# VectorE transposes keys and queries from the 13th chunk; the steps of the inverses read rows; ScalarE scales rows and keys; VectorE makes all low halves

## The chip, the cores and the metric

The kernel runs on one core of one Trainium2 chip. The metric is the device time of one launch in microseconds (us). The engines are called by their names in the profile: PE is TensorE's matmul, PEld its weight load, DVE is VectorE, ACT is ScalarE, POOL is GpSimd, and SP is SyncE, which issues almost all DMAs.

## What is computed

Three layers in fp32: a gated delta rule over 768 steps for 4 batches x 8 heads of width 48, then two dense layers of 384 -> 2048 -> 384 over 3072 tokens, one with mish, one with hardswish.

```
k_n = k / (norm(k) + 1e-06)
for t in range(768):
    y[t]  = q[t] @ state
    v_old = k_n[t] @ state
    state = state + beta[t] * outer(k_n[t], v[t] - v_old)
x = y as (3072, 384)
h = x @ w_in;   x = (h * tanh(softplus(h))) @ w_out
h = x @ w2_in;  out = (h * clip(h + 3, 0, 6) / 6) @ w2_out
```

## The kernel before

**The recurrence** is cut into 24 chunks (t = 0 to 23) of 32 steps; (batch, step) fills the 128 partitions. For a chunk PE transposes keys and queries (`T_pe`, 4 transposes of 128x128 each, into PSUM; `T_ew` on ACT copies them into `kqt`), multiplies keys by keys and keys by queries (`G_pe`, into `gps`), and needs the inverse of the unit lower triangular matrix I + tril(beta K K^T), one 32x32 matrix for each batch and head. Then `rec()` runs, for each chunk in order: K (`ksps`, keys times state), r = v - K on DVE (L942), U (`ups`, inverse times r), its copy on ACT (L986), queries times state and MU (`yps`), S (`dsps`, the state's update) and eight additions into `sbd` on DVE (L890). The products of chunk t + 3 (G) go to PE with K of chunk t, the transposes of chunk t + 4 with U of chunk t.

The inverses of chunks 0 to 7 are made before by two blocks of substitutions (`whole`, `quads`). From chunk 8 on two chunks form a group g (4 to 11): `G_ew` on DVE multiplies the products by a lower mask times -beta (`mb`, made by `beta_mask` on POOL) into `an`; DMAs turn `an` through DRAM (`ad`) so that each partition holds a matrix (`ash`, [128, 32, 32]; its two halves of partitions solve for different columns); `substs` on DVE runs 31 steps, each a product (L785) into `tmp` and an addition (L792) into `tp`; DMAs turn `tp` back through DRAM (`td`) into `pt`, and `scale` on POOL (L813) multiplies `pt` by beta. `ash` and `tp` are single buffers. The upper product (keys by queries) is copied by ACT (`M_post`, L483) and masked by POOL (L622) into `mt`; for chunks 4 to 7 DVE does it from PSUM (`G_ew2`, L478).

**The dense layers** hold each fp32 operand as two halves in fp32r, a high one made by ACT and a low one by DVE (value minus high half), and run three matmuls for each product (`hps` L1205, `o` L1226, `p` L1364). Phase 1 (mish) makes six passes over blocks of 512 tokens, 16 units each; a pass needs four chunks of the recurrence. So phase 1 runs beside chunks 4 to 23. In its first pass the weights are also fetched and split: 28 pieces, for each ACT L1139, DVE L1141, L1144, L1147, L1150, ACT L1167, DVE L1170. The low half of a unit's activations (`glo`, L1245) is made by POOL in the first 16 units and by DVE in the other 80. Phase 2 (hardswish) follows, with no recurrence beside it.

**The order of work** is fixed when the program is built: `Flow` simulates the engines with estimated costs, and each part is a generator that yields either an event it needs or (engine, us). `pen` and `margin` are given by hand; `pen` is added to the part's start when the next instruction is picked. "DVE." marks work that the planner lets run beside POOL; plain "DVE" work it holds back while a POOL instruction runs. Every engine, and SP's queue of DMAs, runs its instructions in that order. PSUM banks are handed out by `room`.

## Time and profile before

| what | before |
|---|---|
| time, median of 3 runs | 1038.77 us (1038.46 to 1041.55) |
| the profiled execution's own time | 1040.45 us |
| its span in the trace | 1038.7 us |
| mean granted TensorE clock | 0.995 |
| PE busy | 1009.0 us (97%) |
| PEld busy | 842.5 us (81%) |
| DVE busy | 655.6 us (63%) |
| ACT busy | 452.0 us (44%) |
| POOL busy | 119.9 us (12%) |

The profiled execution is 1.75 us longer than its span and 1.68 us above the median. Busy time of PE holds overlaps: a matmul of 512 columns is shown as about 0.39 us long, while the next one starts 0.23 us after it, so PE shows as busy whenever its queue is not empty. The other engines' busy time is closer to occupation. The shares are means over a start of 88.5 us, phase 1 beside the recurrence, and phase 2.

### The profile page before, as it was taken

The page shows a single profiled execution, that of the slowest core. Times are in us where ns is not written, and L with a number is a line of the kernel's source. Part 1 is how long each engine was busy: PE and PEld are TensorE (multiplying, and loading weights), DVE is VectorE, ACT ScalarE, POOL GpSimd, SP SyncE. Part 2 cuts the span into 40 slices and gives each one's busy share as a digit, 9 for nine tenths or more (in the row PEclk, how much of TensorE's full clock was granted, in tenths as well). Part 3 has the DMA queues.
Part 4 walks back from the last instruction along what each step waited for, and adds up shares of the span by engine and source line. Part 5 has one row for each costly group of instructions (what it writes and reads, how often), then busy time and mean ns, then how long its engine had stood idle before and what let it go on. Part 6 is the DMA issues. An engine that isn't in the chain of part 4 may idle for free.

```text
span 1038.7 us, 29553 instructions
## 1 busy us (share of the span) xinstructions
PE 1009.0 (97%) x12708; PEld 842.5 (81%) x12730; DVE 655.6 (63%) x1569; ACT 452.0 (44%) x916; POOL 119.9 (12%) x156
## 2 busy tenths in 40 slices
PE   8888999999999999999999999999999999999997
PEld 5466777787777878878778888998999989999997
DVE  7988999976869598596628888333343333433432
ACT  4454666534454354444236665333343333433432
POOL 3242333303121221210000000000000000000000
PEclk9999999999999999999999999999999999999999
DMA  4644553234242434414113643002020020100101
GB/s 87 158 97 103 152 129 99 78 57 77 42 95 41 76 54 87 74 20 89 22 44 121 203 137 107 1 1 62 1 61 1 1 61 1 37 25 1 31 1 32
DMA packets 149124, 66.58 MB, mean 64 GB/s; under 512 B 133088, under 2 KB 136160, under 8 KB 148992
## 3 DMA queue, kind: packets, MB, share of 16 engines
q1 hardware_dynamic: 147664, 64.19, 25.8%
q8 instruction: 100, 1.64, 0.7%
q10 hardware_dynamic: 1328, 0.49, 0.2%
q14 instruction: 32, 0.26, 0.1%
HBM read 51.02 MB, written 13.63 MB: 62 GB/s over the span
## 4 chain that ended last, share of the span: by engine, by line
PE 72%; DVE 16%; issue 2%; ACT 2%; DMA 1%; POOL 0%; SPq 0%; DVEq 0%; ACTq 0%
PE hps L1205 32%; PE p L1364 19%; PE o L1226 12%; DVE tmp L785 3%; DVE sbd L890 3%; DVE tp L792 3%; DVE cv L1147 1%; DVE cv L1150 1%; PE tps L434 1%; PE ksps L827 1%; PE ups L837 1%; PE yps L847 1%; PE dsps L879 1%; PE yps L827 1%; DVE glo L1245 1%
## 5 line engine op out<-in xcount | busy, mean ns | idle before, releaser
L1205 PE MATMUL hps<-xh,wih 128*128 128x512 f32 x576 | 229.5, 398 | 4.7 <-DVE an L472 1.8
L1205 PE MATMUL hps<-xl,wih 128*128 128x512 f32 x576 | 227.5, 395 | 2.3 <-DVE xl L1187 2.2
L1205 PE MATMUL hps<-xh,wil 128*128 128x512 f32 x576 | 227.3, 395 | 0.0
L1339 DVE SCALAR_TENSOR_TENSOR r<-r,hps 128x512 f32<-128x512 f32 x96 | 66.1, 688 | 181.6 <-ACT r L1337 181.4
L1337 ACT ACTIVATE r<-hps,half_c 128x512 f32<-128x512 f32 x96 | 66.1, 689 | 174.8 <-PE hps L1205 174.8
L1205 PEld LDWEIGHTS hps<-xh,wih 128*128 128x128 f32 x576 | 108.7, 189 | 27.5 <-DVE an L472 3.1
L1364 PE MATMUL p<-woh,glo 128*128 128x384 f32 x384 | 129.5, 337 | 0.0
L1364 PE MATMUL p<-woh,ghi 128*128 128x384 f32 x384 | 129.2, 337 | 0.0
L1364 PE MATMUL p<-wol,ghi 128*128 128x384 f32 x384 | 128.9, 336 | 0.0
L1205 PEld LDWEIGHTS hps<-xl,wih 128*128 128x128 f32 x576 | 108.7, 189 | 24.3 <-DVE xl L1187 5.0
L1205 PEld LDWEIGHTS hps<-xh,wil 128*128 128x128 f32 x576 | 108.6, 188 | 23.1
L1236 ACT ACTIVATE g<-hps 128x512 f32<-128x512 f32 x96 | 57.3, 597 | 132.0 <-PE hps L1205 130.2
L1226 PE MATMUL o<-ghi,wol 128*128 128x512 f32 x288 | 114.2, 396 | 0.1
L1226 PE MATMUL o<-ghi,woh 128*128 128x512 f32 x288 | 113.6, 394 | 0.0
L1345 DVE TENSOR_TENSOR glo<-r,ghi 128x512 fp32r<-128x512 f32 x96 | 66.5, 693 | 60.8 <-ACT ghi L1211 60.2
L1245 DVE TENSOR_TENSOR glo<-g,ghi 128x512 fp32r<-128x512 f32 x80 | 56.3, 704 | 75.4 <-ACT ghi L1211 75.0
L1211 ACT ACTIVATE ghi<-r 128x512 fp32r<-128x512 f32 x96 | 60.6, 632 | 70.4 <-DVE r L1339 70.4
L785 DVE TENSOR_TENSOR tmp<-tp,ash 128x126 f32<-128x126 f32 (+22 forms) x248 | 84.8, 342 | 8.8 <-DMA ash<-ad 2.5
L1226 PE MATMUL o<-glo,woh 128*128 128x512 f32 x288 | 84.3, 394 | 0.0
L1364 PEld LDWEIGHTS p<-woh,ghi 128*128 128x128 f32 x384 | 72.2, 188 | 4.0
L1364 PEld LDWEIGHTS p<-wol,ghi 128*128 128x128 f32 x384 | 72.1, 188 | 3.9
L792 DVE TENSOR_TENSOR tp<-tp,tmp 128x126 f32<-128x126 f32 (+22 forms) x248 | 69.3, 279 | 6.5
(148 smaller groups left out, 1384.0 us busy)
## 6 DMA issues: line engine op xcount, KB each, us to landing
raw<-in_moe_w_in_dram SPq DMA_DIRECT2D x24, 512.0 KB, 3.6
raw<-in_moe_w_out_dram SPq DMA_DIRECT2D x32, 384.0 KB, 3.2
vt<-in_v_dram SPq DMA_DIRECT2D x96, 48.0 KB, 2.4
x2d<-x2out SPq DMA_DIRECT2D x6, 768.0 KB, 3.8
x2in<-x2d SPq DMA_DIRECT2D x6, 768.0 KB, 5.5
kpad<-in_k_dram SPq DMA_DIRECT2D x92, 48.0 KB, 2.3
qpad<-in_q_dram SPq DMA_DIRECT2D x88, 48.0 KB, 2.5
ash<-ad SPq DMA_DIRECT2D x16, 256.0 KB, 4.0
```

The costliest lines, as they stand in the source:

```text
L785: nc.vector.tensor_tensor(out=tv, in0=x[:, 0:m, j:j + 1].to_broadcast([128, m, n]), in1=a[:, j + 1:C, j:j + 1].rearrange("p i o -> p o i") ...
L792: nc.vector.tensor_tensor(out=x[:, 0:m, j + 1:C], in0=x[:, 0:m, j + 1:C], in1=tv, op=ALU.add)
L890: nc.vector.tensor_tensor(out=o, in0=o, in1=S_part(b, r), op=ALU.add)
L1205: nc.tensor.matmul(out=ps[0], lhsT=w[:, kk, c], rhs=xhl[n][xi][:, kk, :], start=(kk == 0 and x == 0), stop=(kk == KD - 1 and x == 2))
L1211: nc.scalar.activation(out=hi, in_=g, func=ACTF.Copy)
L1226: nc.tensor.matmul(out=acc[i][dc], lhsT=w[:, e, 128 * dc:128 * (dc + 1)], rhs=a, start=(f == 0 and x == 0), stop=(f == KF - 1 and x == 2))
L1236: nc.scalar.activation(out=g, in_=ps, func=ACTF.Mish)
L1245: (nc.gpsimd if u < KF else nc.vector).tensor_tensor(out=lo, in0=g, in1=hi.bitcast(F32), op=ALU.subtract)
L1337: nc.scalar.activation(out=r, in_=ps, func=ACTF.Relu, scale=1.0 / 6.0, bias=half_c)
L1339: nc.vector.scalar_tensor_tensor(out=r, in0=r, scalar=1.0, in1=ps, op0=ALU.min, op1=ALU.mult)
L1345: nc.vector.tensor_tensor(out=lo, in0=r, in1=hi.bitcast(F32), op=ALU.subtract)
L1364: nc.tensor.matmul(out=acc[n][s], lhsT=a[:, c], rhs=w[:, e, :], start=(f == 0 and x == 0), stop=(f == KF - 1 and x == 2))
```

## The change

From chunk 12 on (`TD`) PE no longer transposes. `loads_q` fetches keys and queries of a chunk a second time (keys are still fetched in the old layout for S), each with four DMAs, into the two buffers `qpad` so that every 32x32 block holds steps by components; `turns` on DVE transposes such blocks, one instruction of 512 elements in each partition for keys and one for queries, straight into `kqt`, whose layout becomes [batch, head pair, 2, 32]. The columns that pad 48 to 64 are set to zero once by two memsets on POOL.

The matrix to be inverted is now I + tril(K K^T) diag(beta). ACT copies the raw product into `an` and multiplies it by beta with one instruction for each head (8, in place); the steps in `substs` read row j of `ash` where they read column j, and subtract; nothing masks `an`. The inverse is not multiplied by beta any more (POOL's L813 goes). Beta enters the upper product instead (POOL's mask becomes upper mask times beta) and the keys that update the state (`scale_k`, 8 instructions of ACT for each chunk, in place, after the chunk's key norms and, below chunk 12, after its transposes; S waits for it). `rec` no longer waits for the mask of chunk t + 3.

The fetch of `ash` moves into a part of its own (`fetches`): once all weights of phase 1 are split, odd groups use another buffer, and `tp` moves to a pool with two buffers. For chunks 4 to 7 the upper product goes to ACT and POOL (`M_early`) instead of DVE. All 96 low halves of phase 1 are made by DVE. Several `pen`s and `margin`s of the planner are set anew, and some cost estimates.

```diff
+        def raw_kq(i):
+            return qpad[i].rearrange("p j r d -> p (j r d)").rearrange("p (n x) -> p n x", x=C)
+
         def loads_q():
-            for t in range(4, NS):
+            for t in range(4, TD):
                 yield f"Tq{t - NQP}"
                 yield LOAD
                 load_q(t)
+            for t in range(TD, NS):
+                yield f"S{t - 5}"
+                for i, src in ((0, k), (1, q)):
+                    yield f"Tq{TD - 2 + i}" if t == TD else f"kqt{t - 1}.{i}"
+                    x = raw_kq(i)
+                    if t == TD:
+                        yield "POOL", 0.5
+                        for r in range(2):
+                            nc.gpsimd.memset(x[64 * r + 32:64 * r + 64, :, 16:32], 0.0)
+                    yield LOAD
+                    for r in range(2):
+                        for d0, d1 in ((0, 32), (32, D)):
+                            nc.sync.dma_start(
+                                out=x[64 * r + d0:64 * r + d0 + C, :, 0:d1 - d0],
+                                in_=src[:, r::2, C * t:C * (t + 1), d0:d1].rearrange("b j s d -> s (b j) d"),
+                            )
+                    flow.ev[f"raw{t}.{i}"] = flow.landed(3.0)
+
+        def turns():
+
+            for t in range(TD, NS):
+                yield f"QS{t - NKQ}"
+                for i in range(2):
+                    yield f"raw{t}.{i}"
+                    yield "DVE.", 0.705
+                    if i == 0:
+                        kqt[t] = ap_.tile([128, B, NP, 2, C], F32, tag=f"kqt{t % NKQ}", name="kqt")
+                    nc.vector.transpose(out=kqt[t].rearrange("p b j i s -> p (b j) i s")[:, :, i, :], in_=raw_kq(i))
+                    flow.set(f"kqt{t}.{i}")
+                flow.set(f"kq{t}")
...
-        def beta_mask(t, tag="mb"):
-            m = ap_.tile([128, H, C], F32, tag=tag, name="mb")
+        def beta_mask(t, tri):
+            m = ap_.tile([128, H, C], F32, tag="mb", name="mb")
             nc.gpsimd.tensor_tensor(
                 out=m,
-                in0=maskl.rearrange("p (o c) -> p o c", o=1).to_broadcast([128, H, C]),
...
-                kqt[t] = ap_.tile([128, NP, B, 2, C], F32, tag=f"kqt{t % NKQ}", name="kqt")
+                kqt[t] = ap_.tile([128, B, NP, 2, C], F32, tag=f"kqt{t % NKQ}", name="kqt")
             nc.scalar.activation(
                 out=kqt[t][:, :, :, i, :],
-                in_=tps.pop((t, i)).rearrange("p j (b s) -> p j b s", b=B),
+                in_=tps.pop((t, i)).rearrange("p j (b s) -> p b j s", b=B),
                 func=ACTF.Copy,
...
-                for r in range(2):
-                    yield "DVE.", 0.28, 0
-                    G_ew2(t, r)
-                    release(("G", t, r))
-                flow.set(f"mt{t}")
+                yield from M_early(t)
...
-            flow.add(M_post(t), pen=-0.227)
+            flow.add(M_post(t), pen=-0.202)
+            g, tt = divmod(t, 2)
+            if tt == 0:
+                an[g] = ap_.tile([128, 2, H, C], F32, tag="an", name="an")
+            x = an[g][:, tt]
             for r in range(2):
-                yield "DVE.", 0.285
-                G_ew(t, r)
+                yield "ACT", 0.28
+                nc.scalar.activation(out=x[:, r::2, :], in_=gps[t, r][:, :, 0:C], func=ACTF.Copy)
                 flow.set(f"an{t}.{r}")
-            if t % 2:
+            yield f"n{t}"
+            for h in range(H):
+                yield "ACT", 0.23, 0
+                nc.scalar.activation(out=x[:, h, :], in_=x[:, h, :], func=ACTF.Copy, scale=bnat[:, t, h:h + 1])
+            if tt:
                 yield "SP", 0.45
-                g = t // 2
                 an[g], x = drp.tile([2 * H, B * C, C], F32, tag="ad", name="ad", bufs=2), an[g]
                 nc.sync.dma_start(out=an[g].rearrange("p s j -> s p j"), in_=x.rearrange("s t h j -> s (t h) j"))
...
                 release(("G", t, r))
+            yield f"mb{t}"
             yield "POOL", 0.74
-            nc.gpsimd.tensor_tensor(out=m, in0=m, in1=masku.rearrange("p (o c) -> p o c", o=1).to_broadcast([128, H, C]),
-                                    op=ALU.mult)
+            nc.gpsimd.tensor_tensor(out=m, in0=m, in1=mbs[t], op=ALU.mult)
             flow.set(f"mt{t}")
+
+        def scale_k():
+
+            for t in range(8, NS):
+                if t < TD:
+                    yield f"Tq{t}"
+                yield f"n{t}"
+                for h in range(H):
+                    yield "ACT", 0.28, 0
+                    x = kdata(t)[:, h, :]
+                    nc.scalar.activation(out=x, in_=x, func=ACTF.Copy, scale=bnat[:, t, h:h + 1])
+                flow.set(f"ks{t}")
         def T_post(t, i):
             yield "ACT", 0.6
             T_ew(t, i)
...
-        def substs():
+        ash = {}
+
+        def fetches():
             for g in range(4, NGR):
                 yield f"ad{g}"
-                yield lock("ash")
+                own = "lo1.27" in flow.ev
+                tag = "r1" if own and g % 2 else "ash"
+                yield lock(tag)
                 yield "SP", 0.9
                 d = an[g].rearrange("p (b s) j -> (p b) (s j)", b=B)
-                a = ap_.tile([128, C, C], F32, tag="ash", name="ash")
-                x = ap_.tile([128, C // 2, C], F32, tag="tp", name="tp")
+                if tag == "r1":
+                    a = cvp.tile([128, 512, 2], F32, tag="r1", name="ash").rearrange("p n t -> p (n t)")
+                    a = a.rearrange("p (s j) -> p s j", j=C)
+                else:
+                    a = ap_.tile([128, C, C], F32, tag="ash", name="ash")
                 for hf in range(2):
                     nc.sync.dma_start(out=a[64 * hf:64 * hf + 64].rearrange("p s j -> p (s j)"), in_=d)
-                at = [flow.landed(2.5)]
+                at = flow.landed(2.5)
+                if own:
+                    x = x2p.tile([128, 512], F32, tag="x2", name="tp").rearrange("p (c i) -> p c i", i=C)
+                else:
+                    x = ap_.tile([128, C // 2, C], F32, tag="tp", name="tp")
                 yield "POOL", 0.75
                 nc.gpsimd.memset(x, 0.0)
                 xf = x.rearrange("p c i -> p (c i)")
                 for hf in range(2):
                     nc.gpsimd.memset(xf[64 * hf:64 * hf + 64, hf::34], 1.0)
-                yield lambda: at[0]
+                ash[g] = a, x, tag
+                flow.ev[f"ash{g}"] = max(at, flow.cur)
+
+        def substs():
+
+            for g in range(4, NGR):
+                yield f"ash{g}"
+                a, x, tag = ash.pop(g)
                 for j in range(C - 1):
                     n, m = C - 1 - j, j // 2 + 1
-                    yield "DVE", 0.165 + 0.00175 * n * m
+                    us = 0.165 + 0.00106 * n * m
+                    yield "DVE", us
                     t = ap_.tile([128, 256], F32, tag="tmp", name="tmp")
                     tv = t[:, 0:m * n].rearrange("p (m n) -> p m n", n=n)
                     nc.vector.tensor_tensor(
-                        out=tv,
-                        in0=x[:, 0:m, j:j + 1].to_broadcast([128, m, n]),
-                        in1=a[:, j + 1:C, j:j + 1].rearrange("p i o -> p o i").to_broadcast([128, m, n]),
-                        op=ALU.mult,
-                    )
-                    yield "DVE", 0.165 + 0.00098 * n * m
-                    nc.vector.tensor_tensor(out=x[:, 0:m, j + 1:C], in0=x[:, 0:m, j + 1:C], in1=tv, op=ALU.add)
-                give("ash")
+                        out=tv, in0=x[:, 0:m, j:j + 1].to_broadcast([128, m, n]),
+                        in1=a[:, j:j + 1, j + 1:C].to_broadcast([128, m, n]), op=ALU.mult)
+                    yield "DVE", us
+                    nc.vector.tensor_tensor(out=x[:, 0:m, j + 1:C], in0=x[:, 0:m, j + 1:C], in1=tv, op=ALU.subtract)
+                give(tag)
                 yield "SP", 0.9
                 d = drp.tile([2 * H, B * C, C], F32, tag="td", name="td", bufs=2)
                 for hf in range(2):
@@ -809,12 +867,6 @@
             yield flow.landed(1.5) - flow.cur
             pt[g] = x
             for t in range(2):
-                yield "POOL", 0.62
-                nc.gpsimd.tensor_tensor(
-                    out=x[:, t], in0=x[:, t],
-                    in1=bnat[:, 2 * g + t, :].rearrange("p (h o) -> p h o", o=1).to_broadcast([128, H, C]),
-                    op=ALU.mult,
-                )
                 flow.set(f"pt{2 * g + t}")
...
-                tk = t + 4 if 4 <= t < NS - 4 else None
+                tk = t + 4 if 4 <= t < TD - 4 else None
...
-                        yield f"mb{tg}"
...
+                if 8 <= t and not last:
+                    yield f"ks{t}"
...
-            yield ("POOL", 1.29) if u < KF else ("DVE", 0.69)
-            (nc.gpsimd if u < KF else nc.vector).tensor_tensor(out=lo, in0=g, in1=hi.bitcast(F32), op=ALU.subtract)
+            yield "DVE", 0.69
+            nc.vector.tensor_tensor(out=lo, in0=g, in1=hi.bitcast(F32), op=ALU.subtract)
...
-            due = flow.ev["moe1"] + 24.438 * (idx // 7) - 2.164 * max(1, end - idx + 1)
-            return 0.025 if due - flow.free["DVE"] < 2.89 else 0.128
+            due = flow.ev["moe1"] + 23.341 * (idx // 7) - 2.164 * max(1, end - idx + 1)
+            return -0.044 if due - flow.free["DVE"] < 2.886 else 0.055
...
-        flow.add(rec(), margin=busy(0.0, 1.05))
+        flow.add(whole(), pen=-0.324)
+        flow.add(rec(), margin=busy(0.0, 0.916))
...
+        flow.add(turns(), pen=0.078)
...
-        flow.add(quads(1), pen=busy(0.305, -0.161), margin=busy(0.0, 1.077))
+        flow.add(scale_k(), pen=busy(0.54, 0.003))
+        flow.add(quads(1), pen=busy(0.251, 0.007), margin=busy(0.0, 1.077))
+        flow.add(fetches(), pen=-0.111)
         flow.add(substs(), pen=0.008)
...
         for _ in range(2):
             flow.add(w1.lane(), pen=w1_pen)
```

## Rows read from the trace of the kernel before

**Rows 1.** The page's head: busy time of the engines.

```profile
PE 1009.0 (97%) x12708; PEld 842.5 (81%) x12730; DVE 655.6 (63%) x1569; ACT 452.0 (44%) x916; POOL 119.9 (12%) x156
```

**Rows 2.** Windows, phase 1's first four passes: us; PE, PEld, DVE, ACT, POOL busy.

```profile
88.50:195.00 106.50, 102.22 (x2105) 80.95 (x2105) 99.27 (x233) 62.19 (x144) 37.63 (x34) 0.98 0.47 123
195.00:290.00 95.00, 92.39 (x1604) 73.66 (x1603) 72.13 (x220) 42.60 (x101) 16.69 (x22) 0.98 0.29 59
290.00:385.00 95.00, 93.18 (x1610) 74.50 (x1609) 70.12 (x222) 41.49 (x101) 18.62 (x23) 1.00 0.36 68
385.00:477.00 92.00, 91.29 (x1610) 74.12 (x1609) 68.49 (x213) 43.40 (x108) 16.33 (x25) 1.00 0.37 70
```

**Rows 3.** Chain of waits by line: stretch 89 to 195, 290 to 385, 385 to 477.

```profile
by line: DVE cv L1147 12.3%; DVE cv L1150 10.7%; issue 10.5%; DVE sbd L890 10.3%; DVE cv L1141 6.3%; DVE wol L1170 6.0%; DVE tmp L785 5.9%; DVE tp L792 5.2%; DVE wil L1170 4.2%; PE hps L1205 3.6%; DVE cv L1144 3.3%; DMA raw<-in_moe_w_in_dra
by line: DVE tmp L785 14.4%; DVE tp L792 12.3%; DVE sbd L890 11.5%; PE hps L1205 11.1%; PE o L1226 9.8%; issue 5.9%; DMA ash<-ad 4.9%; DVE glo L1245 4.6%; POOL nn L414 4.5%; SPq L797 2.1%; ACT vt L342 2.0%; PE ksps L827 1.8%; PE gps L454 1.
by line: PE hps L1205 36.5%; PE o L1226 33.7%; PE tps L434 4.5%; PE dsps L879 3.8%; PE ksps L827 3.7%; PE ups L837 3.5%; PE yps L847 3.5%; PE gps L454 3.4%; PE yps L827 3.0%; PE xps L1041 2.1%; issue 0.7%; DVE tmp L785 0.7%; DVE r L942 0.6%
```

**Rows 4.** Timeline of PE around the transposes of one chunk, near 398 us.

```profile
398.52 0.66 PE L434 MATMUL tps<-ident,kpad 128*128 128x128 f32 x4
399.01 0.60 PE L434 MATMUL tps<-ident,qpad 128*128 128x128 f32 x4
399.37 0.48 PE L1226 MATMUL o<-ghi,wol 128*128 128x512 f32 x1
```

**Rows 5.** Groups by line: busy us, mean ns of one, idle before.

```profile
L785 DVE TENSOR_TENSOR tmp<-tp,ash 128x126 f32<-128x126 f32 (+22 forms) x248 | 84.8, 342 | 8.8 <-DMA ash<-ad 2.5
L792 DVE TENSOR_TENSOR tp<-tp,tmp 128x126 f32<-128x126 f32 (+22 forms) x248 | 69.3, 279 | 6.5
L472 DVE TENSOR_TENSOR an<-gps,mb 128x128 f32<-128x128 f32 x32 | 8.7, 283 | 2.5 <-ACT mt L483 2.5
L440 ACT ACTIVATE kqt<-tps 128x512 f32<-128x512 f32 x48 | 27.1, 595 | 17.8 <-PE tps L434 17.2
L342 ACT ACTIVATE vt<-vt,nn 128x48 f32<-128x48 f32 x144 | 36.2, 322 | 0.6 <-DMA vt<-in_v_dram 0.5
L483 ACT ACTIVATE mt<-gps 128x128 f32<-128x128 f32 x40 | 9.1, 272 | 34.8 <-PE gps L454 34.8
L1245 POOL TENSOR_TENSOR glo<-g,ghi 128x512 fp32r<-128x512 f32 x16 | 23.4, 1462 | 47.3 <-ACT ghi L1211 36.4 <-issue 10.9
L1245 DVE TENSOR_TENSOR glo<-g,ghi 128x512 fp32r<-128x512 f32 x80 | 56.3, 704 | 75.4 <-ACT ghi L1211 75.0
L641 DVE STREAM_TRANSPOSE late<-late 128x1024 f32<-128x1024 f32 x1 | 1.2, 1246 | 0.0
L718 DVE STREAM_TRANSPOSE late<-late 128x1024 f32<-128x1024 f32 x1 | 1.9, 1929 | 0.0
```

**Rows 6.** Timeline of POOL and DVE near 94 to 98 us.

```profile
94.61 1.29 POOL L1245 TENSOR_TENSOR glo<-g,ghi 128x512 fp32r<-128x512 f32 x1 [6.07 <-ACT ghi L1211]
94.79 1.53 DVE L1150 SCALAR_TENSOR_TENSOR cv<-raw,cv 128x384 uint32<-128x384 uint32 x1
98.07 0.55 DVE L1150 SCALAR_TENSOR_TENSOR cv<-raw,cv 128x384 uint32<-128x384 uint32 x1
```

**Rows 7.** Timeline of ACT: seven instructions of the value scaling in a row.

```profile
333.03 1.68 ACT L342 ACTIVATE vt<-vt,nn 128x48 f32<-128x48 f32 x7
```

**Rows 8.** Chain of waits in order of time, from 301 to 309 us.

```profile
301.16 1.36 SPq L797
...
304.02 4.61 DMA ash<-ad
```

**Rows 9.** Timeline of SP: four DMAs of one chunk's queries.

```profile
225.41 1.80 SPq L268 DMA_DIRECT2D qpad<-in_q_dram  x4
```

**Rows 10.** Timeline of POOL and ACT: an inverse scaled, then the copy of U.

```profile
218.60 1.19 POOL L813 TENSOR_TENSOR pt<-pt,bnat 128x256 f32<-128x256 f32 x2 [3.25 <-DMA pt<-td]
223.63 0.49 ACT L986 ACTIVATE u<-ups 128x384 f32<-128x384 f32 x1 [2.98 <-PE ups L837]
```

More of the change, by code (lines that the diff above doesn't have):

```diff
@@ L21 @@
 NKQ = 4
+TD = 12
 RATE, TOKENS = 32.0, 110.0
@@ L553, in matrix @@
             yield "POOL", 0.62
-            beta_mask(t)
+            beta_mask(t, maskl)
             yield 0.05
@@ L827, in state_pe @@
                     nc.tensor.matmul(
-                        out=ps[C * b:C * (b + 1), j, :], lhsT=kqt[t][:, j, b, i, :], rhs=sbd[:, b, j, :],
+                        out=ps[C * b:C * (b + 1), j, :], lhsT=kqt[t][:, b, j, i, :], rhs=sbd[:, b, j, :],
                         start=(i == 0 or j == 0), stop=(i == 0), skip_group_check=True,
@@ L932, in rec @@
                         G_pe(tg)
-                        flow.add(G_post(tg), pen=0.029, back=0.4 if tx and x1 else 0.0)
+                        flow.add(G_post(tg), pen=0.046, back=0.4 if tx and x1 else 0.0)
                     if tx and x1:
@@ L1577, in tile_delta_rule__moe_mish__moe_hardswish @@
             flow.add(w1.lane(), pen=w1_pen)
-        flow.add(moe(), pen=0.292)
+        flow.add(moe(), pen=0.321)
         flow.add(phase2())
```

31 lines of the change are left out of this document (13 added, 18 removed).

## The prediction

> **What bounds the kernel now.** I read the head of the page first, then busy time by stretch, then the chain of waits, then PE's timeline. The head shows PE busy for 97% of the span and no other engine above 63% [rows 1]. A mean hides the stages, so the next view cuts phase 1 at the starts of its passes [rows 2]. In the first pass PE is idle for 106.50 - 102.22 = 4.3 us and DVE for 106.50 - 99.27 = 7.2 us: both are nearly full. In the second to fourth pass, 282 us, PE is idle for 282 - 276.86 = 5.1 us, DVE for 71 us, ACT for 154 us. The chain of waits says who sets the pace [rows 3]: in the first pass it runs over DVE's splitting of weights (L1147, L1150, L1141, L1170), in the third largely over DVE's inverse steps (L785, L792) and state additions (L890) with PE's dense matmuls between, in the fourth over PE almost alone, and 4.5% of that stretch are the transposes (L434) that the change removes. So from 195 us on PE is full, with the inverses close behind; before that DVE is.
>
> **PE's transposes.** They go for chunks 12 to 23, 12 blocks of 8. One block goes from 398.52 to the next matmul at 399.37, 0.85 us from start to start [rows 4]; its busy time would count overlaps. 12 x 0.85 = 10.2 us. All 12 blocks stand beside U of chunks 8 to 19, in the stretch where PE is full. The dense matmuls behind them move up, so I take the whole 10.2 us; the bounds are nothing (if another engine sets the pace) and 10.2.
>
> **What DVE gets in return.** Two transposes of 512 elements for each of 12 chunks. The trace has none of this shape; 1024 dense elements take 1.25 us, and 1.93 us where one side is strided [rows 5]. Half of the dense one is 0.62, the full strided one 1.93; I take 0.70, near the dense row, since blocks of 32 stay dense: 24 x 0.70 = 16.8 us, at most 46. Against it stand the two products of each chunk into `an` (L472, 0.283), 32 x 0.283 = 9.1 us, and the step's product, which by reading rows should cost what the addition costs: 248 x (342 - 279) ns = 15.6 us [rows 5]; the bounds are nothing and that. From 195 to 477 us this is about 24 x 0.70 - 24 x 0.283 - 13.7 = -3.7 us for DVE. It lies in DVE's 71 us of idle time; even at 1.93 each (+26 us) it would fit. Without that cover it would cost what it takes.
> The row on PE's side is 0.85 us for a chunk's transposes, on DVE's side about 1.4 us, and ACT's two copies of 0.595 us go too [rows 4, 5]. The Trainium skill ("VectorE: DVE Perf Modes", Rules for kernel authors) speaks against the change: for a full 128x128 transpose it says to use TensorE where PSUM will do as destination. By that rule the sum would lose, 16.8 us for 10.2; by the rows it gains, because PE is the full engine after 195 us and DVE is not.
>
> **The inverses.** Between two groups DVE had no step to run: after one group's result is written (1.36 us of SP) the next fetch of `ash` takes 4.61 us, both on the chain [rows 8]. With two buffers the fetch is early. The scaling of the result on POOL also goes, 1.19 us for two, and U comes some 5 us after it starts [rows 10]. So pauses and late inverses become rarer; what is late next is PE itself. I give half of PE's 5.1 us of idle time in these passes as regained, 2.5 us; bounds 0 and 5.1.
>
> **ACT.** Each chunk from 8 on gets 2 copies of 0.272 us (L483's shape), 8 scalings of 128x32 and 8 of 128x48. The latter shape takes 0.322 us alone, but seven in a row take 1.68 us, (1.68 - 0.322) / 6 = 0.226 us apart [rows 5, 7]. For 128x32 the bounds are 0.15 (by elements) and 0.322; I take 0.226. A chunk: 2 x 0.272 + 2 x (7 x 0.226 + 0.322) = 4.35 us. From 195 to 477 us 13 chunks add 56.6 us and 24 copies of 0.595 go (14.3): 42 on 127.5, so 170 of 282 us. It is hidden by ACT's idle time. New waits: S waits for the scaled keys, U's copy can queue behind a run of 1.9 us; PE has dense matmuls for such a time, so I cost it at nothing, and at 1.9 us for each chunk if it has none.
>
> **The first pass.** DVE gets 16 low halves of 0.704 us, 11.3 us; it loses the 8 products of chunks 4 to 7 and the 6 of chunks 8 to 10 (0.283 each, 4.0 us) [rows 5]. That is +7.3 us on 99.27, the whole stretch. But POOL's 16 low halves, 23.4 us, also slowed DVE: the same instruction (L1150) took 1.53 us beside one and 0.55 us later [rows 6]. The relief is between nothing and 16 x 0.98 = 15.7 us; I take half, 7.8, as not every POOL half met such work. Net -0.5 us of DVE: nothing. ACT there gets 8 x 0.272 + 3 x 4.35 = 15.2 us on 62.19. I count the first pass as unchanged; bounds: 4.3 us shorter (PE's idle time) to 22 us longer (below).
>
> **SP's queue and DMA.** For chunks 12 on eight DMAs replace the four of the queries. Four take 1.80 us of SP, 0.45 each [rows 9], so four more make +1.8 us for each chunk; at 1.36 each, as one of a write of `td` took [rows 8], +9.1. Behind them in SP's order stand the transfers of the inverses, keys and values. A chunk lasts some 24 us (95 / 4), so I cost it at nothing. POOL's masks change in kind only; two memsets come once.
>
> **Sum.** -10.2 - 2.5 + 0 = -12.7 us. The profiled execution took 1040.45 us in all, its span and 1.75 us around it; it would take 1027.75. That execution lies 1.68 us above the median, so for the median 1038.77 - 12.7 = 1026.1 us. Start, last passes and phase 2 are left as they are: PE alone fills phase 2.
>
> **Rivals.** *More is regained.* The inverses no longer hold anything up and the first pass loses its 4.3 us: -10.2 - 5.1 - 4.3 = -19.6, 1019.2 us. For it speaks the chain in the third pass and the first; against it that PE's idle time is spread over many small waits. Chance 0.15.
> *SP falls behind.* If the short rows of keys and queries make each DMA cost 1.36 us of SP, 12 chunks are each delayed by up to 9.1 us in their inverses; PE covers most of it with dense matmuls until the block of tokens runs out at a pass's end. At about 1.5 us in each of four passes it gives back 6 us and nothing is regained: 1038.77 - 10.2 + 6 = 1034.6. Against it: 0.45 is what such DMAs take. Chance 0.13.
> *TensorE is not the bound.* The chain of the third pass runs more over DVE than over PE [rows 3]; if the inverses' loop sets the pace, PE waits where it transposed, and only the regained 2.5 us are left: 1036.3 us, no change. Against it: PE's idle time is only 5.1 of 282 us, and in the fourth pass the chain is PE. The Trainium skill ("Perfetto Trace Analysis", Identifying the Most-Contended Engine) bears on this: matmul busy time overstates how full TensorE is, the share of weight loads tells better. PEld is busy for 222.3 of these 282 us, 79% [rows 2], and by that rule PE has a fifth to spare and the rival holds; no row here shows such spare time as waits. Chance 0.09.
> *The first pass gets longer.* The place is ACT and DVE between 88.5 and 195 us, where the chain is DVE's splitting of weights with ACT at both its ends. If there is no relief from POOL, DVE needs 106.6 us and keeps its 7.2 us of waits: +7.3; if the 15.2 us of small ACT instructions also stand ahead of the splitting, the pass grows by up to 22 us: 1038.77 - 10.2 + 22 = 1050.6. It decides once the pass grows by more than 10.2 + 3.1. For it: both engines' work grows where they are the chain; against it: ACT has 44 us of idle time there, and the POOL row. Chance 0.08.
>
> **How the numbers follow.** The forecast as summed, 1021 to 1031.5 us, has 0.55; the rivals 0.15, 0.13, 0.09 and 0.08. A measurement here can tell 0.3%, 3.1 us. Faster: 0.55 + 0.15 + 0.13 = 0.83; same 0.09; slower 0.08. The range for 8 in 10 takes in the first two rivals: 1018 to 1036.
>
> **What would show it.** PE's L434 should lose 96 instructions and the time from the start of the second pass to that of the fifth should shrink by 10 us or more; L785's mean should equal L792's; DVE transposes should take about 0.70 us; in the first pass L1150 should have no instruction near 1.5 us beside a low half. Wrong would be: the chain of the second to fourth pass moving to ACT's scalings or SP's issues, PE waiting for `kqt`, or a first pass well over 106 us.

## The result, and the profile after

The changed kernel takes 1026.4 us (median of 4 runs, 1024.99 to 1028.12), the kernel before in the same comparison 1040.16 us; the ratio is 0.9863, 95% interval 0.9828 to 0.9899. In a second comparison it was 0.9882 (0.9854 to 0.9910). That is 12.3 to 14.2 us (the two intervals together reach from 9.4 to 17.9), and 1026.1 us was forecast. The forecast's sum held; the experiments below show that its terms did not all hold. A trace shows a single execution, which can lie some us off its kernel's median (in two of the experiments below, 1042.0 against 1037.34 us in e5 and 1045.9 against 1043.81 in e4), so lengths of passes read from one trace are good to some us only.

The head of the page of the changed kernel, which answers to [rows 1]:

```profile
span 1023.5 us, 29655 instructions
PE 996.6 (97%) x12620; PEld 831.4 (81%) x12620; DVE 640.6 (63%) x1569; ACT 496.4 (49%) x1188; POOL 88.3 (9%) x132
```

The shares hardly move; only ACT gains (452.0 to 496.4 us) and POOL loses (119.9 to 88.3). Where the time went is seen by passes. A pass is here taken from ACT's first high half of its block of tokens to that of the next, the first pass from the first dense matmul. Busy time of the changed kernel's first five passes (us; PE, PEld, DVE, ACT, POOL; then the granted clock, DMA share and GB/s), which answers to [rows 2]:

```profile
83.70:189.90 106.20, 100.75 (x2204) 79.23 (x2201) 100.11 (x252) 80.12 (x238) 21.52 (x27) 0.98 0.48 126
189.90:281.10 91.20, 89.17 (x1579) 71.20 (x1578) 67.13 (x213) 51.20 (x158) 15.15 (x21) 1.00 0.42 75
281.10:370.20 89.10, 88.71 (x1581) 71.22 (x1580) 69.23 (x224) 54.03 (x174) 14.03 (x19) 1.00 0.47 82
370.20:461.40 91.20, 89.49 (x1582) 72.14 (x1581) 65.39 (x203) 50.24 (x156) 11.55 (x16) 1.00 0.42 74
461.40:544.80 83.40, 83.40 (x1229) 67.39 (x1229) 51.84 (x138) 34.04 (x61) 0.00 (x0) 1.00 0.20 62
```

Cut in the same way, the kernel before starts its first dense matmul at 89.0 us and its passes take 103.2, 97.2, 94.7, 92.8 and 83.9 us:

```profile
89.00:192.20 103.20, 99.09 (x2078) 78.74 (x2075) 96.63 (x224) 60.31 (x140) 36.79 (x32) 0.98 0.48 125
192.20:289.40 97.20, 94.50 (x1612) 74.95 (x1611) 74.17 (x225) 43.88 (x105) 17.31 (x22) 0.98 0.29 57
289.40:384.10 94.70, 92.88 (x1609) 74.27 (x1608) 69.92 (x221) 41.19 (x101) 17.89 (x24) 1.00 0.35 67
384.10:476.90 92.80, 92.09 (x1613) 74.80 (x1612) 69.29 (x216) 44.20 (x108) 17.23 (x25) 1.00 0.37 70
476.90:560.80 83.90, 83.63 (x1230) 67.26 (x1229) 52.04 (x132) 32.71 (x59) 3.28 (x4) 1.00 0.18 52
```

So the start is 5.3 us earlier, the first pass 3.0 us longer, the second to fourth are 6.0, 5.6 and 1.6 us shorter (13.2 together, where 10.2 + 2.5 were forecast), the fifth 0.5; the rest differs by 0.8 us the other way.

About 1.7 us of the second pass's 6.0 are TensorE's clock. In the kernel before PE is busy for only 1.31 and 1.19 of 2 us in the stretches from 194 and 196 us, and in the next two, from 198 to 202 us, the granted clock is 0.52 and 0.62, near the lower of its two levels (1.00 is 2.4 GHz, 0.50 is 1.2 GHz); 2 x 0.48 + 2 x 0.38 = 1.7 us is an estimate of what that costs. In the changed kernel the granted clock is 1.00 in every such stretch from 100 to 490 us. So here a wait of TensorE at a pass's end was followed by a loss of about its own size.

The chain of waits by line in the first pass (84 to 190 us) and the third (281 to 370 us) of the changed kernel, which answers to [rows 3] (the view ends its lines where they end here):

```profile
by line: PE hps L1258 19.1%; PE o L1279 15.4%; PE qps L776 6.2%; DVE sbd L942 5.2%; issue 4.7%; DVE cv L1203 4.1%; DVE cv L1200 3.7%; POOL nn L448 3.7%; ACT an L638 3.2%; ACT kqt L474 2.4%; PE gps L488 2.3%; DVE wil L1223 2.2%; ACT wih L122
by line: PE hps L1258 35.8%; PE o L1279 33.2%; PE ksps L879 3.6%; PE gps L488 3.5%; DVE sbd L942 3.1%; PE dsps L931 2.9%; PE yps L899 2.7%; PE ups L889 2.7%; DVE tp L850 2.2%; PE yps L879 2.2%; PE xps L1094 2.2%; DVE tmp L846 1.7%; issue 1.
```

The third pass was DVE's (inverse steps 14.4% and 12.3%) and is now PE's: the steps have 1.7% and 2.2%. In the first pass DVE's splitting of weights (L1200 and L1203, before L1147 and L1150) falls from 23% to 8%, PE's dense matmuls (L1258, before L1205) rise from 3.6% to 19.1%, and ACT's scalings (L638) appear.

Groups by line (busy us, mean ns of one, idle before), which answer to [rows 5]: PE's transposes before, then the changed kernel:

```profile
L434 PE MATMUL tps<-ident,kpad 128*128 128x128 f32 x100 | 16.6, 290 | 0.0
L434 PE MATMUL tps<-ident,qpad 128*128 128x128 f32 x88 | 13.5, 275 | 0.7 <-DVE r L942 0.7
```

```profile
L468 PE MATMUL tps<-ident,kpad 128*128 128x128 f32 x52 | 9.9, 318 | 0.2
L468 PE MATMUL tps<-ident,qpad 128*128 128x128 f32 x40 | 6.1, 276 | 0.0
L354 DVE STREAM_TRANSPOSE kqt<-qpad 128x512 f32<-128x512 f32 x24 | 17.0, 707 | 0.1
L846 DVE TENSOR_TENSOR tmp<-tp,ash 128x126 f32<-128x126 f32 (+22 forms) x248 | 65.6, 264 | 12.5 <-POOL tp L831 4.3 <-DMA ash<-ad 2.1
L850 DVE TENSOR_TENSOR tp<-tp,tmp 128x126 f32<-128x126 f32 (+22 forms) x248 | 65.7, 265 | 7.1
L666 ACT ACTIVATE kpad<-kpad,bnat 128x48 f32<-128x48 f32 x128 | 32.1, 324 | 17.0 <-DVE bnat L416 17.0
L1298 DVE TENSOR_TENSOR glo<-g,ghi 128x512 fp32r<-128x512 f32 x96 | 66.6, 694 | 66.2 <-ACT ghi L1264 65.5
```

The prices were right: a transpose on DVE takes 0.707 us (0.70 forecast), the step's product costs as much as its partner (264 and 265 ns), a scaling of the keys 0.324 us. PE's transposes fall from 100 to 52 for keys and from 88 to 40 for queries, 96 in all. The longest instruction of the weights' splitting (L1203, before L1150) falls from 1.67 to 1.31 us, where none near 1.5 us was expected.

ACT's timeline (six scalings of 128x32, then eight of 128x48) and SP's (the new loads of one chunk) in the second pass:

```profile
227.23 1.37 ACT L638 ACTIVATE an<-an,bnat 128x32 f32<-128x32 f32 x6
232.08 1.92 ACT L666 ACTIVATE kpad<-kpad,bnat 128x48 f32<-128x48 f32 x8 [3.11 <-DVE bnat L416]
```

```profile
237.20 2.93 SPq L339 DMA_DIRECT2D qpad<-in_k_dram  x4
240.23 2.66 SPq L339 DMA_DIRECT2D qpad<-in_q_dram  x4
```

A run of eight takes 1.92 us, as summed; the narrower ones come (1.37 - 0.325) / 5 = 0.21 us apart, 0.325 being the median of one alone. A DMA of the new kind takes SP 0.67 to 0.73 us in this chunk and 0.48 to 0.86 over all 12 chunks, between the 0.45 taken and the bound of 1.36. The chunk's transposes on DVE (L354) have 0.1 us of idle time before them in all, so the loads are early enough.

### The profile page after: what moved, and what is told of

Its sections match the earlier page's. It is cut to its first block, busy times and chain, and to the rows that moved or that the text cites. A ratio compares the mean times of both kernels' runs of the same rounds, so it can differ in the third digit from the quotient of the medians.

```text
span 1023.5 us, 29655 instructions
## 1 busy us (share of the span) xinstructions
PE 996.6 (97%) x12620; PEld 831.4 (81%) x12620; DVE 640.6 (63%) x1569; ACT 496.4 (49%) x1188; POOL 88.3 (9%) x132
## 4 chain that ended last, share of the span: by engine, by line
PE 85%; DVE 10%; ACT 3%; issue 2%; POOL 0%; DMA 0%; SPq 0%; DVEq 0%; ACTq 0%
PE hps L1258 37%; PE p L1417 20%; PE o L1279 17%; PE dsps L931 2%; PE ups L889 1%; PE ksps L879 1%; PE gps L488 1%; DVE sbd L942 1%; PE yps L899 1%; DVE tw L700 1%; PE yps L879 1%; DVE late L707 1%; PE xps L1094 1%; DVE tmp L846 1%; DVE cv L1200 1%
## 5 line engine op out<-in xcount | busy, mean ns | idle before, releaser
L1258 PE MATMUL hps<-xh,wih 128*128 128x512 f32 x576 | 229.5, 399 | 2.6 <-ACT mt L510 1.3
L1258 PE MATMUL hps<-xh,wil 128*128 128x512 f32 x576 | 226.7, 394 | 0.7 <-issue 0.7
L1258 PE MATMUL hps<-xl,wih 128*128 128x512 f32 x576 | 226.5, 393 | 0.0
L1258 PEld LDWEIGHTS hps<-xh,wih 128*128 128x128 f32 x576 | 108.4, 188 | 26.6 <-issue 2.7
L1258 PEld LDWEIGHTS hps<-xh,wil 128*128 128x128 f32 x576 | 108.3, 188 | 23.2
L1258 PEld LDWEIGHTS hps<-xl,wih 128*128 128x128 f32 x576 | 108.4, 188 | 19.2
L1298 DVE TENSOR_TENSOR glo<-g,ghi 128x512 fp32r<-128x512 f32 x96 | 66.6, 694 | 66.2 <-ACT ghi L1264 65.5
L1398 DVE TENSOR_TENSOR glo<-r,ghi 128x512 fp32r<-128x512 f32 x96 | 66.5, 693 | 60.8 <-ACT ghi L1264 60.3
L846 DVE TENSOR_TENSOR tmp<-tp,ash 128x126 f32<-128x126 f32 (+22 forms) x248 | 65.6, 264 | 12.5 <-POOL tp L831 4.3
L1417 PEld LDWEIGHTS p<-woh,glo 128*128 128x128 f32 x384 | 72.0, 188 | 0.0
```

The costliest lines, as they stand in the source:

```text
L846: nc.vector.tensor_tensor(out=tv, in0=x[:, 0:m, j:j + 1].to_broadcast([128, m, n]), in1=a[:, j:j + 1, j + 1:C].to_broadcast([128, m, n]), ...
L1258: nc.tensor.matmul(out=ps[0], lhsT=w[:, kk, c], rhs=xhl[n][xi][:, kk, :], start=(kk == 0 and x == 0), stop=(kk == KD - 1 and x == 2))
L1298: nc.vector.tensor_tensor(out=lo, in0=g, in1=hi.bitcast(F32), op=ALU.subtract)
L1398: nc.vector.tensor_tensor(out=lo, in0=r, in1=hi.bitcast(F32), op=ALU.subtract)
L1417: nc.tensor.matmul(out=acc[n][s], lhsT=a[:, c], rhs=w[:, e, :], start=(f == 0 and x == 0), stop=(f == KF - 1 and x == 2))
```

## The experiments

Two theories were set against each other. *Theory 1* is the forecast's: from the second pass on TensorE alone sets the pace, so its transposes are worth their time. *Theory 2* was formed after the first four runs: a pass ends when both are done, TensorE's work and the recurrence with the inverses and low halves that pass through VectorE's queue, and the two were about equally long before. All ratios are to the kernel before in the same comparison; differences from the changed kernel use its two ratios, 0.9863 and 0.9882, with 0.1% = 1.04 us. Each of these ratios has an interval of about 3 us to either side, so a difference under some 4 us is not clear of noise.

**The changed kernel again (e1).** No edit.

> The changed kernel once more, as the base of the others. Theory and rivals alike: about 14 us under the kernel before, the second to fourth pass 3 to 6 us shorter each.

1027.89 us, ratio 0.9882 (0.9854 to 0.9910); passes of 107.4, 90.3, 90.1, 90.8 and 83.3 us. The gain and its place repeat.

**All transposes on TensorE, and half of them.**

```diff
-TD = 12
+TD = 24      # e2;  18 in e3
```

> The changed kernel with TensorE making the transposes of chunks 12 to 23 as well (TD = 24); all else is as changed. Theory (TensorE sets the pace from the second pass on, so its transposes are worth their own time): 12 x 0.85 = 10.2 us slower than the changed kernel, some 3.4 us in each of the second, third and fourth pass. Rival (the inverses or ScalarE set the pace, and TensorE only waits where it transposed): within 3 us of the changed kernel.

> The changed kernel with TensorE making the transposes of chunks 12 to 17 (TD = 18), half of what e2_all_on_tensor does. Theory: 6 x 0.85 = 5.1 us slower than the changed kernel, in the second and third pass, the fourth unchanged. Rival: within 3 us, or no relation to the number of transposes.

e2: 1033.27 us, 0.9938 (0.9915 to 0.9961), 5.4 us above the changed kernel in the same comparison; e3: 1033.0 us, 0.9929 (0.9903 to 0.9955), 5.1 us above. The time of e3 fits the forecast, though its fourth pass, forecast as unchanged, is 2.3 us longer (93.5 us); all transposes together cost half of their forecast. There is no line through both, so neither the forecast nor its rival holds as stated. The planner chose another order in both; in e2 one chunk of the recurrence moved from the fifth pass to the fourth or before, and the time to phase 2 is 617.5 us against 610.1.

**Only the turn (e4).** The kernel before with `TD`, `raw_kq`, the new `loads_q`, `turns` and the layout of `kqt`, and nothing else of the change:

```diff
-                tk = t + 4 if 4 <= t < NS - 4 else None
+                tk = t + 4 if 4 <= t < TD - 4 else None
...
+        flow.add(turns(), pen=0.078)
```

> The kernel before with only one part of the change: VectorE transposes keys and queries from chunk 12 on (with the layout and the loads that this needs). Low halves, inverse steps, masks, scalings and buffers are as before. Theory: 10.2 us faster than the kernel before, or 8 to 10 if the inverses, which keep their slow products and single buffer, take back a little. Rival (the inverses are as close behind as TensorE, and only their relief made room): 0 to 4 us faster.

1043.81 us (12 runs), 1.0027 (1.0006 to 1.0049): not 10.2 us faster, so theory 1 falls here. That the turn itself costs time is not shown: the mean granted clock of these 12 executions is 0.9906, that of the 19 of the kernel before 0.9947, and among each kernel's own executions 0.001 of clock goes with about 0.8 us. At an equal clock the two kernels come out within 1 us of each other (an estimate, from a straight line through each kernel's executions). In the trace the second pass starts at 195.1 us, 2.9 us later than before the change, when VectorE has not yet made a single turn (the first is at 227.2 us). The planner also made a new order. The passes take 97.0, 96.1 and 94.1 us from the second to the fourth, where the kernel before took 97.2, 94.7 and 92.8:

```profile
195.10:292.10 97.00, 92.93 (x1597) 74.21 (x1596) 76.92 (x232) 40.01 (x97) 16.78 (x23) 1.00 0.37 64
292.10:388.20 96.10, 91.53 (x1581) 72.51 (x1580) 74.50 (x228) 38.01 (x93) 17.16 (x23) 0.98 0.41 71
388.20:482.30 94.10, 90.43 (x1579) 71.90 (x1578) 71.50 (x218) 38.20 (x94) 17.05 (x23) 0.98 0.41 67
```

PE is idle in them for 4.1, 4.6 and 3.7 us, 12.3 in all against 5.2 before: most of TensorE's saved time became waiting, and another 1.7 us went because the clock fell in two passes where it had fallen in one (0.50 to 0.66 from 298 to 302 us, 0.50 and 0.77 from 394 to 398 us, each time after a wait at the start of a pass). The passes don't hold quite the same work: the trace has 77 matmuls fewer in them than before, not 96. The list of PE's waits of this run (195 to 566 us; us in total, times, longest) and the timeline at the start of the third pass name the place:

```profile
PE hps L1240 <- DVE xl L1222: 8.9, 5, 3.3
```

```profile
291.54 0.49 ACT L1092 ACTIVATE xst<-xps 128x384 f32<-128x384 f32 x1
...
292.07 0.64 ACT L1218 ACTIVATE xh<-xst 128x512 fp32r<-128x512 f32 x1
...
295.85 0.68 DVE L1222 TENSOR_TENSOR xl<-xst,xh 128x512 fp32r<-128x512 f32 x1
...
296.58 0.50 PE L1240 MATMUL hps<-xl,wih 128*128 128x512 f32 x1 [3.32 <-DVE xl L1222]
```

The recurrence hands over the last columns of the block at 291.54, the high half follows at once, but the low half waits in DVE's queue until 295.85 behind steps of the next inverse and other work, and PE waits 3.32 us. Two things are late at the same point: the recurrence ends just when TensorE has run out of the block before, and DVE is busy. A part may be the loads: the chain of the third pass holds loads of keys for 3.9% (2.06 and 1.69 us), which neither the kernel before nor the changed one has there. No run separates that.

**The other side: slow steps again (e5).** In the changed kernel, every engine's order kept:

```diff
-                        in1=a[:, j:j + 1, j + 1:C].to_broadcast([128, m, n]), op=ALU.mult)
+                        in1=a[:, j + 1:C, j:j + 1].rearrange("p i o -> p o i").to_broadcast([128, m, n]), op=ALU.mult)
```

> The changed kernel with the steps' product reading column j of the matrix, as before, where the change reads row j; the order on every engine is the same as in the changed kernel. (The numbers of the inverses are other ones: the scaling by beta stands on the wrong side, so the output is not the reference's.) Theory 2 (a pass ends when both TensorE's work and the recurrence with its inverses are done, and the relief of the inverses is what lets TensorE's 10.2 us count): each product about 0.08 us longer, 31 x 0.08 = 2.4 us for a group, 4.8 us for the two groups of a pass; 3 to 10 us slower than the changed kernel in all, with TensorE waiting for the next block's low halves at the ends of passes. Theory 1 (TensorE alone sets the pace): 0 to 2 us slower.

1037.34 us (12 runs), 0.9984 (0.9972 to 0.9995): 10.6 to 12.6 us above the changed kernel, nearly all of its gain and more than expected, though PE has none of its transposes back. Groups and the first two passes of this run:

```profile
L846 DVE TENSOR_TENSOR tmp<-tp,ash 128x126 f32<-128x126 f32 (+22 forms) x248 | 81.7, 330 | 15.3 <-POOL tp L831 5.2 <-DMA ash<-ad 3.9
```

```profile
83.70:194.70 111.00, 103.12 (x2207) 80.68 (x2203) 101.57 (x252) 80.46 (x238) 21.49 (x27) 0.97 0.47 121
194.70:291.40 96.70, 92.72 (x1584) 73.23 (x1584) 71.98 (x214) 51.19 (x158) 15.06 (x21) 0.98 0.40 70
```

The products take 81.7 - 65.6 = 16.1 us more in all; the first pass is 4.8 us longer and the second 5.5, although DVE is idle for 9.4 and 24.7 us in them. That idle time is no cover. (The trace is the longest of the 12 executions, 4.7 us above their median, so the passes show the place rather than the size; 1.7 us of the second are a fall of the clock to 0.52 and 0.63 at 230 to 234 us, after a wait.) Theory 1's 0 to 2 us is out. Theory 2 has the direction right, with an effect above its 3 to 10 us, but the waits are mostly not where it put them: in the second pass PE waits for 0.4 us for the next block's low halves, and for 3.1 us for DVE's additions to the state (L942). The longest of these waits, 2.10 us, ends at 228.81 us, in mid pass; the additions begin at 227.97 us, behind two turns, slow steps and a low half in DVE's queue. So what counts is that DVE's queue is late, at a pass's end or before it.

**Single buffers (e6).** `own` false throughout:

```diff
-                own = "lo1.27" in flow.ev
+                own = False
```

> The changed kernel with one buffer for the fetched matrix and one for the inverse throughout, as before. Theory 2: a group's fetch again starts only when the group before is done, some 6 us (1.36 + 4.61) without steps for each of six groups; 4 to 12 us slower than the changed kernel, in the second to fourth pass, with waits of TensorE at the ends of passes. Theory 1: 0 to 2 us slower.

1028.95 us, 0.9899 (0.9875 to 0.9924): 1.8 to 3.7 us above the changed kernel, with overlapping intervals. The third and fourth pass are 3.1 and 1.4 us longer. At most a small part of the gain; less than theory 2 gave it.

**Low halves on GpSimd.** The line of the kernel before, first with the planner's own price (e7), then with the price and so the order of the changed kernel (e11):

```diff
-            yield "DVE", 0.69
-            nc.vector.tensor_tensor(out=lo, in0=g, in1=hi.bitcast(F32), op=ALU.subtract)
+            yield ("POOL", 1.29) if u < KF else ("DVE", 0.69)      # e7 only; e11 keeps ("DVE", 0.69)
+            (nc.gpsimd if u < KF else nc.vector).tensor_tensor(out=lo, in0=g, in1=hi.bitcast(F32), op=ALU.subtract)
```

> The changed kernel with GpSimd making the low halves of the first 16 units, as before. As predicted (the 11.3 us that VectorE gets are given back by less contention): the first pass within 2 us of the changed kernel's. Rival (these halves are why the changed kernel's first pass is 3 us longer than before, 106.2 against 103.2 us): first pass 3 us shorter, total 3 us faster.

> As e7_low_halves_on_gpsimd, but the order of the other engines stays that of the changed kernel, so that only the place of the 16 low halves differs. If e7's long first pass (117.3 us) came from the order that the planner chose: first pass within 3 us of the changed kernel's 106.2. If it comes from the halves themselves (GpSimd takes 1.46 us for one where VectorE takes 0.70, and slows VectorE beside it): 5 to 11 us longer.

e7: 1033.54 us, 0.9946 (0.9931 to 0.9960), first pass 117.3 us. e11: 1031.62 us, 0.9925 (0.9901 to 0.9950), first pass 111.9 us against 106.2 and 107.4. So neither of e7's two expectations held, the pass is longer: 5.7 or 4.5 us come from the halves themselves, and 5.4 us of e7's from its order. Groups of e11, then the same lines of the changed kernel:

```profile
L1298 POOL TENSOR_TENSOR glo<-g,ghi 128x512 fp32r<-128x512 f32 x16 | 22.5, 1408 | 50.9 <-ACT ghi L1264 43.8 <-issue 7.1
L1203 DVE SCALAR_TENSOR_TENSOR cv<-raw,cv 128x384 uint32<-128x384 uint32 x16 | 11.8, 744 | 0.1
L1203 DVE SCALAR_TENSOR_TENSOR cv<-raw,cv 128x512 uint32<-128x512 uint32 x12 | 11.5, 962 | 0.1
```

```profile
L1203 DVE SCALAR_TENSOR_TENSOR cv<-raw,cv 128x512 uint32<-128x512 uint32 x12 | 9.4, 780 | 0.0
L1203 DVE SCALAR_TENSOR_TENSOR cv<-raw,cv 128x384 uint32<-128x384 uint32 x16 | 8.7, 550 | 0.0
```

One line of the splitting alone takes 23.3 us beside GpSimd's halves and 18.1 us without them. DVE is busy for 105.88 us in e11's first pass although it has 15 halves less to make there, and for 100.11 us in the changed kernel's: the relief, 105.88 - 100.11 + 10.4 = 16.2 us, is larger than the halves' own 15 x 0.694 = 10.4 us.

**VectorE applies beta (e8).** In the changed kernel, in `G_post`:

```diff
-                yield "ACT", 0.28
-                nc.scalar.activation(out=x[:, r::2, :], in_=gps[t, r][:, :, 0:C], func=ACTF.Copy)
...
-                yield "ACT", 0.23, 0
-                nc.scalar.activation(out=x[:, h, :], in_=x[:, h, :], func=ACTF.Copy, scale=bnat[:, t, h:h + 1])
+                yield "DVE.", 0.285
+                nc.vector.tensor_tensor(
+                    out=x[:, r::2, :], in0=gps[t, r][:, :, 0:C],
+                    in1=bnat[:, t, r::2].rearrange("p (h o) -> p h o", o=1).to_broadcast([128, NP, C]), op=ALU.mult)
```

> The changed kernel with VectorE multiplying the products by beta out of PSUM, two instructions for each chunk, in place of ScalarE's two copies and eight scalings. ScalarE loses 2 x 0.272 + 1.9 = 2.45 us for each of 16 chunks, VectorE gets 0.57. Theory 2: the matrices leave some 2 us earlier for the inverses, but VectorE has more to do; within 2 us of the changed kernel. Rival (ScalarE's small instructions are what lengthens the first pass): first pass 2 to 3 us shorter. Rival (VectorE is so close behind that 0.57 us for each chunk count): 3 to 9 us slower.

1033.94 us, 0.9946 (0.9934 to 0.9958): 6.7 to 8.6 us above the changed kernel. The second to fifth pass (89.7, 89.0, 90.5, 83.2 us) are as short as the changed kernel's; all of the loss is a first pass of 116.8 us. e7's first pass was as long with another edit, and half of that was its order, so this run doesn't say whether six more products on DVE or the planner's new order did it.

**Transposes on TensorE, order kept.** In the changed kernel, 96 transposes added (e9); in the kernel before, the 96 left out (e10):

```diff
             ps = bank(("U", t), [128, H, D], "ups")
+            if 8 <= t < NS - 4:
+                for i in range(8):
+                    nc.tensor.transpose(ps.rearrange("p h d -> p (h d)")[:, 0:128],
+                                        kp(t)[:, i % NP].rearrange("p r d -> p (r d)"), ident)
```

```diff
+            if t >= 12:
+                ps = src.rearrange("p j r d -> p j (r d)")
+            else:
                 for j in range(NP):
                     nc.tensor.transpose(ps[:, j, :], src[:, j].rearrange("p r d -> p (r d)"), ident)
```

> The changed kernel, each engine's order kept, with 96 transposes that nobody uses added to TensorE where the kernel before has them (eight with U of chunks 8 to 19, into the bank that U then fills). Theory 2 and theory 1 alike: in the changed kernel TensorE sets the pace from the second pass on, so all of 96 x 0.106 = 10.2 us come back. Rival (the inverses still set the pace in part): 5 us or less come back.

> The kernel before, each engine's order kept, without the 96 transposes of chunks 12 to 23: ScalarE copies the untransposed keys and queries instead, so the output is not the reference's. Theory 2: nothing on TensorE's side is worth its time while the inverses are as they were: 0 to 4 us faster, TensorE waiting at the ends of passes. Theory 1: 10.2 us faster.

e9: 1033.25 us, 0.9932 (0.9911 to 0.9954), 5.2 to 7.2 us above the changed kernel. e10: 1038.03 us (12 runs), 0.9978 (0.9961 to 0.9995), 2.3 us below the kernel before. Second to fourth pass of e9, then of e10, then PE's waits of e10 (190 to 560 us):

```profile
191.40:284.20 92.80, 92.12 (x1612) 74.99 (x1611) 67.24 (x213) 51.40 (x158) 15.12 (x21) 1.00 0.43 73
284.20:377.80 93.60, 92.39 (x1614) 75.25 (x1613) 69.50 (x224) 54.68 (x175) 14.03 (x19) 1.00 0.44 78
377.80:470.40 92.60, 91.93 (x1613) 75.24 (x1612) 66.06 (x206) 50.53 (x157) 11.64 (x16) 1.00 0.42 73
```

```profile
193.20:288.10 94.90, 90.99 (x1579) 71.29 (x1578) 73.29 (x224) 43.36 (x104) 17.31 (x22) 1.00 0.31 58
288.10:382.80 94.70, 90.60 (x1576) 71.35 (x1575) 70.18 (x222) 41.20 (x101) 18.70 (x24) 1.00 0.35 67
382.80:474.30 91.50, 89.50 (x1581) 71.90 (x1580) 69.29 (x216) 43.97 (x109) 17.12 (x25) 1.00 0.37 70
```

```profile
PE ksps L830 <- DVE sbd L893: 3.9, 10, 0.5
PE hps L1208 <- DVE xl L1190: 3.1, 5, 0.8
PE hps L1208 <- DVE an L475: 2.5, 3, 1.0
```

In the changed kernel's order the 96 transposes are worth 279.0 - 271.5 = 7.5 us of the three passes, in the order of the kernel before 284.7 - 281.1 = 3.6 us, of which 1.7 are the fall of the clock that only the trace of the kernel before has in these passes. There PE's idle time rises from 5.2 to 10.0 us (3.9, 4.1 and 2.0), and nearly all of it is waiting for DVE. Theory 1's 10.2 us is out in e10, and theory 2's 0 to 4 us holds; e9 is short of the 10.2 us that both gave. The intervals of the two totals (0.5 to 4.1 us in e10, about 3 to 9 in e9) touch; that the transposes are worth more in the changed kernel rests on the passes, and on e2 and e5 set against the kernel before (in the part on the prediction).

**The planner's numbers of before (e12).** The changed kernel with all penalties, margins and due times set back, for example:

```diff
-        flow.add(whole(), pen=-0.324)
-        flow.add(rec(), margin=busy(0.0, 0.916))
+        flow.add(whole(), pen=-0.22)
+        flow.add(rec(), margin=busy(0.0, 1.05))
```

> The changed kernel with the planner's penalties, margins and due times of the kernel before; the new parts keep theirs. If the gain is that of the operations: within 4 us of the changed kernel, the first dense matmul later (89 in place of 83.7 us). Rival (the gain needs the order that the new numbers give): 8 us or more slower than the changed kernel, mostly in the first pass.

1030.93 us, 0.9914 (0.9888 to 0.9939): 3.3 to 5.3 us above the changed kernel. The first pass of this run:

```profile
89.20:195.10 105.90, 98.38 (x2134) 78.98 (x2132) 96.13 (x239) 76.95 (x220) 23.91 (x26) 0.97 0.50 126
```

It is as long as the changed kernel's, but starts at 89.2, where the kernel before starts. So the earlier start is the numbers', and with the old numbers the second pass begins at 195.1 us, 2.9 us later than before the change. Most of the gain is left (0.9914), and the loss is below the rival's 8 us or more, so the gain is mainly that of the operations.

## Why the prediction was right, and where its steps were not

The forecast of 1026.1 us was met, with 13.2 us in the second to fourth pass where 12.7 were summed. The runs show that this agreement is luck in part: TensorE was taken as the one engine that sets the pace, and terms were off in both directions.

*PE's transposes.* The working took "the whole 10.2 us". Measured are 7.5 us in the changed kernel's passes (e9), 3.6 us in the kernel before (e10). By the whole time it is 5.2 to 7.2 us (e9) and 2.3 us (e10). The step failed at "the dense matmuls behind them move up": they do so until the block of tokens is used up, and the next block's halves come through the recurrence and DVE.

*What DVE gets in return.* The prices held. That they would vanish in "DVE's 71 us of idle time" did not hold: the turn alone gained nothing (e4), where taking the transposes from PE alone had gained 0.22% (e10), and 16.1 us more of steps cost 10.6 to 12.6 us (e5). DVE's idle time stands largely ahead of low halves that wait for ACT (45.2 of the 71 us, L1245 between 192 and 477 us), at places fixed by the order; work put ahead of such a place can delay it. The rule of the Trainium skill weighed there ("VectorE: DVE Perf Modes", Rules for kernel authors), to transpose 128x128 on TensorE where PSUM will do, is on full transposes; the change's loads bring blocks of 32x32, and only these are turned. Alone the turn gains nothing (e4), beside the other edits 5.4 us (e2), so these runs neither bear the rule out nor speak against it.

*The inverses.* 2.5 us were given to them, with DVE's shorter products counted as covered. e5 takes only the row reading back and loses 10.6 to 12.6 us. This is the term most undersized. The double buffer, named as a cause of the regained time, is worth 1.8 to 3.7 us (e6), not clear of noise.

*"TensorE is not the bound".* This rival had 0.09 and gave 1036.3 us. As a statement on the kernel before it was the better one: the turn alone is no gain. It lost because the change also relieves the inverses, by far more than the 2.5 us that this rival, like the sum, gave to them. The section that was set beside it (Trainium skill, "Perfetto Trace Analysis", Identifying the Most-Contended Engine) holds matmul busy time a poor measure of how close TensorE is to its limit and goes, beside the arithmetic done, by the weight loads' share instead. That matmul busy time overstates is the working's own reading, of matmuls shown 0.39 us long and started 0.23 us apart. The 97% did not settle the matter, but the share of the weight loads does not settle it either: in the second to fourth pass it is 79% in both kernels, and the fifth left over is not seen as waits in either (PE is idle for 5.2 of 284.7 us before and 4.1 of 271.5 after).

*The first pass.* "Unchanged" came out as 3.0 us longer from its own start, and 2.3 us earlier at its end. The relief from POOL was put at half of its bound, net nothing; order kept, the move makes that pass 4.5 to 5.7 us shorter (e11). That the pass is longer all the same must come from the rest; ACT's busy time there rises from 60.3 to 80.1 us and its scalings stand in the chain, but e8, meant to show it, changed the order as well. This stays open.

*The start.* It was "left as it is". The new planner's numbers make it 5.3 us earlier (e12), a part of the diff that the working had passed over.

*ACT, SP.* Right: in the second to fourth pass ACT has 26 us more (129.3 to 155.5; 42 were summed) and they are hidden, SP's loads are in time, and the rival "SP falls behind" did not come.

The single effects don't add up to the gain: taking back the transposes costs 5 to 7 us, the row reading 11 to 13, the low halves 4 to 6, the planner's numbers 3 to 5, together more than the 12 to 14 us won. Against the kernel before, the change without the turn gains 0.62% or 6.5 us (e2, in an order of its own), without the row reading 0.16% or 1.7 us (e5), and with both 12.3 to 14.2 us, more than the two together. That is what one expects where a pass ends with the later of two: each edit taken back alone makes the other side the last to be done.

## What to carry to other kernels

Where two resources finish a stage within a few us of each other, time taken from one is worth little until the other is relieved too: here 2.3 of 10.2 us alone, 5 to 7 beside the relief. An engine's idle time in a fixed order is not cover: ask whether the work lies ahead of something that the busy engine waits for, and test a step's price by putting it back with every engine's order kept, since a planner that orders anew moved a single pass by 5 us here.

## What the runs showed of the hardware

A product on VectorE whose second operand steps by 32 elements (128 bytes) took 387 ns for 126 elements, and 291 ns with neighbouring elements, at the same place in the same order. Groups by form of e5, then of the changed kernel:

```profile
L846 DVE TENSOR_TENSOR tmp<-tp,ash 128x126 f32<-128x126 f32 x24 | 9.3, 387 | 0.6
```

```profile
L846 DVE TENSOR_TENSOR tmp<-tp,ash 128x126 f32<-128x126 f32 x24 | 7.0, 291 | 0.6
```

VectorE's bitwise instructions on two operands in SBUF (L1203, 128x384) took 744 ns on average where GpSimd made 16 subtractions of 128x512 in the same stretch, and 550 ns where it didn't (e11 and the changed kernel, above).

TensorE's granted clock fell after waits at the ends of passes. In e4 PE waited 3.32 us until 296.58 us; the granted clock was 0.50 from 298 to 300 us and 0.66 from 300 to 302 us (0.50 is the level of 1.2 GHz), and dense matmuls that had started 0.22 us apart (296.92 and 297.14 us) then started 0.43 us apart (298.11 and 298.54 us).
